# Page slots chosen by readiness, one page more, and the gated half's idle tags put to use, in a two-layer linear-attention and gMLP kernel

## The chip, the core and the metric

The program runs on one core of a Trainium2 chip. The core has a matrix engine (TensorE, PE in the profile; its weight loads are PEld), three elementwise engines (VectorE or DVE, ScalarE or ACT, GpSimd or POOL), a sync engine (SP) that mostly issues DMAs, and 16 DMA engines. Each engine takes its instructions in order; semaphores hold an instruction back until what it needs is done, and whoever stands behind it on that engine waits too. Matmuls write to PSUM (8 banks); all other tiles lie in SBUF.

The metric is the device time of one execution in microseconds, here the median of several runs.

## The reference

Two layers, each an attention block (A) and a gated MLP block (B), all in float32, on 2048 tokens of 512 features:

```python
def _A_ref(x, wqkv, wo):                       # 32 heads of 16
    q, k, v = split(x @ wqkv)
    phi = lambda t: where(t > 0, t + 1, exp(t)) + 1e-6
    pq, pk = phi(q), phi(k)
    kv = einsum("bhsd,bhse->bhde", pk, v)
    z = einsum("bhsd->bhd", pk)
    num = einsum("bhqd,bhde->bhqe", pq, kv)
    den = einsum("bhqd,bhd->bhq", pq, z)[..., None] + 1e-6
    return (num / den) merged @ wo

def _B_ref(x, w_in, w_sp, b_sp, w_out):        # 1792 = 2 x 896 hidden features
    z = gelu(x @ w_in)
    z1, z2 = z[..., :896], layernorm(z[..., 896:])
    g = einsum("ts,bsf->btf", w_sp, z2) + b_sp[None, :, None]
    return (z1 * g) @ w_out

x = x + _A_ref(layernorm(x)); x = x + _B_ref(layernorm(x))   # twice
```

## The kernel before

**Arithmetic.** Every operand of a large product is split into a high part (an ACT copy to fp32r, `high`, L133) and a low part (a DVE subtraction, `low`, L136), and a product is three matmuls (`mm3`, L147 to L149). The big product with `w_sp` (2048 x 2048) and parts of the product with `w_in` are done with fewer products by block sums, so sums and differences of blocks of `w_sp` and `w_in` have to be made; they depend on the weights alone and are stored in DRAM.

**Tokens.** The 2048 tokens are 16 tiles of 128 (`NT`), and each stage runs over them in steps `s` or `i`.

**Stages of a layer.** `P1` (layer norm, keys, the sum G over tokens, queries), `transition` (the 16 x 16 head matrices folded into one 512 x 512 matrix), `P2` (called the gated half below: attention output, residual, layer norm, the first MLP product with gelu, layer norm of its second half), then `P4` (the product with `w_sp`, the gate, the product with `w_out`). The first layer's P1 (`first`) loads and normalises x; the second's (`second`) gets rows that P4 has normalised.

**Rows turned through DRAM.** Matmuls need the features on the partitions. Class `Turn` does this for most tiles by a store to DRAM (L313), a load in another order (L317, by way of L129) and a DVE transposition into a fresh page (L328).

**SBUF slots.** `main` holds 22 pages (`pg`, 128 x 512 floats each), 6 quads, 4 bigs, and 16 tags `z0` to `z15`, one for each token tile. A z tag carries the tile's queries from P1 to P2 (read last by `a2_mul(i)`, in P2's step i − 2), and from P2's step i + 3 on its gelu output z (`e2`). In between nothing is in it. `Slots` hands pages out as a queue: `put` appends a slot to the end of the free list in program order, `get` takes the slot at its head (L48), whatever was done to it last. The tile framework adds the waits: whoever writes into a slot waits for everything that still reads or writes its last content, a store's landing included. `put` comes right behind the emission of a page's last use, for a store right behind the issue of its DMA.

**A step of the gated half** (`P2.run`, from L1074) emits for its engines in this order from step 7 on: loads of x and of a turned row of the attention output (SP); `b_high(s)` and `b_low(s)`, which take three pages, y (L328), h (L133) and l (L136); `c`, a product (TensorE), `c2` (DVE, L835), `c_stats` (DVE, then three small GpSimd operations L266, L267, L271); `a2_mul`; `c3` (ACT normalise, L277, into a fresh page, then a turn through DRAM); `a` (GpSimd); `d_high` and `d_low` (the turned row split into a quad, ACT L133 and DVE L136 on qd); `e4`, `e(s − 3)` (24 matmuls on 448 columns) and `e2` (gelu, L893), `e3` (statistics), up to two `f()` (12 matmuls each, gelu L918, store L921), `side`, and then in the first layer

- `make.step(s)`: class `Make` builds the block sums of `w_in` in three groups, group g beginning at step `MAKE_AT[g]`: fetch (two loads), one step later `add` (four DVE operations, L213 to L216), then two splits and four stores (L228) to `win1_sums`;
- `sums.tick(s, TOKEN_TICKS)`: class `Sums` builds sums of `w_sp` blocks: three loads one step ahead, three GpSimd additions (L1188) at a tick, three stores (L1183) one step later. Eight of them fall into the first layer's gated half, the others into P4 (`MIX_TICKS`).

The second layer's gated half has neither; it runs `Inner.staged` there, block sums inside a block of `w_sp`, on DVE and ACT.

**A step of the first layer's keys** (`P1.first`, from L576): loads, `x_high`, `T_high` (takes y, h), `K` (12 matmuls), `x_low`, `T_low` (l), `K_phi` (r), for ten steps also `Q` (12 matmuls), one or two pieces of the side weights, `K_high`, `Inner.staged` in `ROW_UNITS`, `K_low` (L436), which adds r into the running sum zacc on GpSimd (L440) and gives the old zacc's page back (L441), then `ln_b`, and `Gmm(s − 2)` (12 matmuls), which gives four pages back.

**Constants.** `ident`, `mask` (block diagonal, loaded at the start by L503) and `ones` are tiles of their own; `ones` is the stationary operand of the start's warm-up matmuls (L511) and of the sum over tokens of zacc in `transition` (L705), `mask` is used there too (L726).

Of the kernel before, what the change touches and what calls it, by code (L numbers as in the profile page):

```python
# [36 lines left out]
class Slots:  # L37


    def __init__(self, pool, prefix, n):  # L40
        self.pool, self.prefix = pool, prefix
        self.free_list = deque(range(n))
        self.held = {}
        self.count = 0

    def get(self, shape, dtype=F32):
        assert self.free_list, f"no {self.prefix} slot"
        n = self.free_list.popleft()  # L48
# [5 lines left out]
    def put(self, *tiles):  # L54
        for t in tiles:
            n, _ = self.held.pop(id(t))
            self.free_list.append(n)


class Views:  # L60
# [14 lines left out]
    def put(self, t):  # L75
        if id(t) not in self.held:
            self.pages.put(t)
            return
# [7 lines left out]
def mixer_kernel(ctx: ExitStack, tc: tile.TileContext, x_in, wqkv, wo_d, win1_d, win2_d, wsp_d, bsp_d, wout_d,  # L86
# [9 lines left out]
    pages = Slots(main, "pg", 22)  # L96
# [17 lines left out]
    nc.vector.tensor_copy(ones, ones_f)  # L114
# [36 lines left out]
    class Weight:  # L151
# [13 lines left out]
        def piece(self, pool=False, lows=None):  # L165
# [15 lines left out]
            if lows is None:  # L181
                split(h, l, src, pool)
                pages.put(r)
# [17 lines left out]
    class Make:  # L201
# [22 lines left out]
        def store(self, g):  # L224
# [4 lines left out]
            pages.put(p, l)  # L229
# [103 lines left out]
    class P1:  # L333
# [28 lines left out]
        def send(self, i):  # L362
# [4 lines left out]
            pages.put(self.y)  # L367
# [65 lines left out]
        def K_low(self, i):  # L433
# [5 lines left out]
            else:  # L439
                nc.gpsimd.tensor_tensor(r, self.zacc, r, op=OP.add)  # L440
                pages.put(self.zacc)  # L441
# [50 lines left out]
        def start(self):  # L492

            nc.gpsimd.affine_select(ident, ones_f, pattern=[[1, P]], compare_op=OP.is_equal, fill=0.0, base=0,
# [11 lines left out]
            nc.vector.tensor_copy(m, f)  # L506
            b = banks.get(PAGE)

            def idle(n):
                for _ in range(n):  # L510
                    nc.tensor.matmul(b, ones, m, start=True, stop=True)  # L511
# [17 lines left out]
            pages.put(m, f)  # L529
# [41 lines left out]
        def first(self, side):  # L571
# [3 lines left out]
            own.home = Views(pages, *spare)  # L575
            for s in range(1, NT + 2):  # L576
# [56 lines left out]
        def second(self, side):  # L633
# [4 lines left out]
            for s in range(1, NT + 2):  # L638
# [41 lines left out]
                if s >= 4 and side:  # L680
                    side[0].fetch()
                if s == NT - 1:
                    own.home.close()
# [7 lines left out]
    def transition(p1, p2):  # L691
        wv, wo = p1.wv, p1.wo
        zh, zl = pages.get(PAGE, F32R), pages.get(PAGE, F32R)
# [3 lines left out]
        pages.put(za)  # L697
# [38 lines left out]
        pages.put(m)  # L736
# [1157 lines left out]
```

## Time and profile before

| what | us |
|---|---|
| median of 3 runs (1389.72 to 1391.08) | 1390.81 |
| the profiled execution | 1388.77 |
| its span, first to last instruction | 1387.1 |
| TensorE busy | 1365.0 |
| from the first layer's start to its head matrices (zb, L705) | 135.8 |
| its gated half, with the head matrices | to 371.0 |
| its P4 | to 715.1 |
| the second layer's keys | to 835.6 |
| its gated half, with the head matrices | to 1050.9 |
| its P4, to the end | to 1387.1 |

In the profile, `pg`, `qd`, `bg`, `bank` are pages, quads, bigs and PSUM banks, `z_q` and `z_z` are z tags with queries and with z; `s`, `z`, `n`, `x`, `qt`, `yt`, `xt`, `win_sums` are DRAM tiles (block sums, gelu output, inner sums, x, turned rows of three kinds, sums of `w_in`). `out<-in` names what an instruction writes and reads. A wait `A <- B` reads: A could start only when B was done. `SPq` and the like are an engine's sequencer, which issues DMAs and waits. A matmul's duration there is modelled from its start; the spacing of starts tells the rate.

### The profile page before, as it was taken

What the parts mean: (1) busy time and instruction counts of PE and PEld (TensorE: products, weight loads), DVE (VectorE), ACT (ScalarE), POOL (GpSimd) and SP (SyncE); (2) the same over time, 40 slices, a digit from 0 to 9 for tenths busy, and PEclk for the clock granted to TensorE, in tenths of its full rate; (3) what the DMA queues carried; (4) which work ended last, traced back from release to release, by engine and by line L of the source; (5) the groups of instructions that cost most, each with busy time, mean ns of one, the idle gap of its engine ahead of it and who ended that gap; (6) DMA issues with size and microseconds to landing.
All of it is one profiled execution on the core that took longest, in us unless ns stands there. A gap on an engine that the chain in (4) does not pass through costs nothing.

```text
span 1387.1 us, 18361 instructions
## 1 busy us (share of the span) xinstructions
PE 1365.0 (98%) x6087; PEld 1132.7 (82%) x6087; DVE 1032.3 (74%) x1581; ACT 638.2 (46%) x1021; POOL 470.4 (34%) x551
## 2 busy tenths in 40 slices
PE   9999999988999999999999999999999999999998
PEld 7877888777778888888888888888888888888887
DVE  6885897666765889996578767977776799878742
ACT  6775544344453343343356655543455534533410
POOL 2333474434324325534531124633240011312250
PEclk9999999999999999999999999999999999999999
DMA  5673377876687898896677542666567798658652
GB/s 184 198 217 117 93 242 246 267 236 206 221 280 271 287 316 260 285 330 229 218 248 229 180 150 65 206 200 221 184 205 252 243 333 320 211 187 301 233 183 90
DMA packets 184352, 310.11 MB, mean 224 GB/s; under 512 B 15680, under 2 KB 67776, under 8 KB 180160
## 3 DMA queue, kind: packets, MB, share of 16 engines
q1 hardware_dynamic: 172592, 262.66, 57.5%
q0 software_dynamic: 8064, 39.85, 8.2%
q10 hardware_dynamic: 3600, 6.42, 1.2%
q8 instruction: 48, 0.79, 0.2%
q14 instruction: 48, 0.39, 0.1%
HBM read 211.62 MB, written 97.26 MB: 223 GB/s over the span
## 4 chain that ended last, share of the span: by engine, by line
PE 75%; DVE 8%; DMA 6%; ACT 5%; issue 2%; POOL 2%; SPq 1%; ACTq 0%; DVEq 0%; POOLq 0%
PE bank L149 11%; PE bank L147 11%; PE bank L148 11%; PE bank L1595 9%; PE bank L1596 9%; PE bank L1594 9%; PE bank L1527 3%; PE bank L1528 3%; PE bank L1525 3%; DVE st L262 1%; DVE pg L136 1%; DVE pg L328 1%; PE bank L983 1%; PE bank L985 1%; PE bank L984 1%
## 5 line engine op out<-in xcount | busy, mean ns | idle before, releaser
L1595 PE MATMUL bank<-qd,pg 128*128 128x512 f32 x544 | 211.7, 389 | 0.8 <-DVE qd L1441 0.8
L1596 PE MATMUL bank<-qd,pg 128*128 128x512 f32 x544 | 211.6, 389 | 0.0
L1594 PE MATMUL bank<-qd,pg 128*128 128x512 f32 x544 | 211.6, 389 | 0.0
L1441 DVE TENSOR_TENSOR qd<-qd,qd 128x1024 fp32r<-128x1024 f32 x104 | 142.6, 1372 | 66.2 <-ACT qd L1432 66.0
L1432 ACT ACTIVATE qd<-qd 128x1024 fp32r<-128x1024 f32 x104 | 110.3, 1060 | 127.5 <-DVE qd L1441 45.7
L133 ACT ACTIVATE pg<-pg 128x512 fp32r<-128x512 f32 (+1 forms) x146 | 90.2, 622 | 142.7 <-DVE pg L328 41.9
L149 PE MATMUL bank<-qd,pg 128*128 128x512 f32 x380 | 149.6, 394 | 0.8 <-DVE pg L136 0.8
L1188 POOL TENSOR_TENSOR pg<-pg,pg 128x512 f32<-128x512 f32 x64 | 94.6, 1478 | 137.4 <-DMA pg<-in_wsp_dram 118.1
L266 POOL TENSOR_SCALAR rs<-mv 128x1 f32<-128x1 f32 x95 | 42.1, 444 | 286.6 <-DVE mv L264 274.9
L1616 POOL TENSOR_TENSOR bg<-bg,pg 128x512 f32<-128x512 f32 x56 | 91.1, 1638 | 109.0 <-DMA pg<-z 61.9
L277 ACT ACTIVATE pg<-pg,nb,rs 128x512 f32<-128x512 f32 x63 | 51.3, 815 | 162.0 <-POOL nb L271 161.7
L136 DVE TENSOR_TENSOR pg<-pg,pg 128x512 fp32r<-128x512 f32 (+1 forms) x143 | 106.5, 745 | 22.7 <-ACT pg L133 13.6
L1595 PEld LDWEIGHTS bank<-qd,pg 128*128 128x128 f32 x544 | 102.1, 188 | 22.6 <-DVE qd L1441 1.2
L1594 PEld LDWEIGHTS bank<-qd,pg 128*128 128x128 f32 x544 | 102.1, 188 | 21.4
L1596 PEld LDWEIGHTS bank<-qd,pg 128*128 128x128 f32 x544 | 102.1, 188 | 20.9
L147 PE MATMUL bank<-qd,pg 128*128 128x512 f32 x284 | 111.1, 391 | 0.6 <-ACT pg L133 0.6
L148 PE MATMUL bank<-qd,pg 128*128 128x512 f32 x284 | 110.6, 390 | 0.0
L147 PE MATMUL bank<-bg,qd 128*128 128x448 f32 x256 | 95.6, 374 | 8.5 <-ACT qd L133 8.5
L328 DVE STREAM_TRANSPOSE pg<-pg 128x512 f32<-128x512 f32 x79 | 85.9, 1087 | 17.5 <-DMA z<-pg 6.1
L149 PE MATMUL bank<-bg,qd 128*128 128x448 f32 x256 | 95.4, 373 | 0.2
L148 PE MATMUL bank<-bg,qd 128*128 128x448 f32 x256 | 94.8, 370 | 0.0
L149 PEld LDWEIGHTS bank<-qd,pg 128*128 128x128 f32 x380 | 71.3, 188 | 21.0 <-DVE pg L136 6.4
(214 smaller groups left out, 3235.9 us busy)
## 6 DMA issues: line engine op xcount, KB each, us to landing
qd<-s SPq DMA_DIRECT2D x64, 512.0 KB, 4.0
qd<-n POOLq DMA_DIRECT2D x32, 1024.0 KB, 7.9
pg<-in_wsp_dram SPq DMA_DIRECT2D x95, 256.0 KB, 4.6
qd<-in_wsp_dram SPq DMA_DIRECT2D x40, 512.0 KB, 4.3
s<-pg SPq DMA_DIRECT2D x64, 256.0 KB, 4.4
pg<-z SPq DMA_DIRECT2D x56, 256.0 KB, 3.9
n<-pg SPq DMA_DIRECT2D x54, 256.0 KB, 4.4
x<-pg SPq DMA_DIRECT2D x48, 256.0 KB, 2.6
```

Source lines behind the costliest of these rows:

```text
L136: nc.vector.tensor_sub(l, src, h.bitcast(F32))
L147: nc.tensor.matmul(out, ah, bh, start=start, stop=False)
L148: nc.tensor.matmul(out, ah, bl, start=False, stop=False)
L149: nc.tensor.matmul(out, al, bh, start=False, stop=stop)
L328: nc.vector.transpose(y.rearrange("p c (t m) -> p m c t", m=4), r.rearrange("p (m c j) -> p m c j", m=4, c=4))
L1188: nc.gpsimd.tensor_tensor(t, a, b, op=OP.add)
L1432: nc.scalar.activation(wh, r, AF.Copy)
L1441: nc.vector.tensor_sub(wl, r, wh.bitcast(F32))
L1594: m(out, h[:, o], w[:, 0, j, :], start=start, stop=False, skip_group_check=True)
L1595: m(out, h[:, o], w[:, 1, j, :], start=False, stop=False, skip_group_check=True)
L1596: m(out, l[:, o], w[:, 0, j, :], start=False, stop=stop, skip_group_check=True)
L1616: nc.gpsimd.tensor_tensor(u, u, z1, op=OP.mult)
```

## The change

Five things.

1. **Slots by readiness.** The free list holds pairs (count, slot). `put` files a slot under the number of gets so far plus a lag: 0 where an engine other than GpSimd used it last, `POOL` = 3 where GpSimd reads it, `STORE` = 6 where a store does. `get` takes the lowest number.
2. **One page more**, 23; to make room `mask`, `ones` and `ones_f` are no longer tiles of their own, and `den` rotates over 2 buffers rather than 4. The warm-up matmuls use slices of one page of ones; `mask` and `ones` get two pages late in P1, step 15, where the mask is loaded and, in step 16, the ones are made from it by one DVE operation; `transition` gives both back.
3. **Block-sum operands in idle z tags.** `TOKEN_TICKS` becomes a dictionary from the step to the tags that the operands of its sum take; what has no tag takes a page.
4. **Turned rows in idle z tags.** `c3(i)` normalises into tag z[i − 1] rather than into a page where the row is turned through DRAM; both layers.
5. **Times.** The last two sums of the gated half move from steps 14 and 17 to 13 and 14; `MAKE_AT` from 7, 10, 12 to 5, 8, 11; the inner sums of the first layer's keys begin before step 1 and run in steps 1 to 8; the second side piece a step begins at step 9 rather than 10.

```diff
-TOKEN_TICKS = (5, 6, 8, 9, 11, 12, 14, 17)
+STORE, POOL = 6, 3
+TOKEN_TICKS = {5: (5, 6), 6: (7,), 8: (8, 9), 9: (10,), 11: (11, 12), 12: (13,), 13: (14,), 14: (15,)}
-MAKE_AT = 7, 10, 12
-ROW_UNITS = range(2, 10)
+MAKE_AT = 5, 8, 11
+ROW_UNITS = range(1, 9)
...
-        self.free_list = deque(range(n))
+        self.free_list = [(0, i) for i in range(n)]
...
-        n = self.free_list.popleft()
+        first = min(self.free_list, key=lambda e: e[0])
+        self.free_list.remove(first)
+        n = first[1]
...
-    def put(self, *tiles):
+    def put(self, *tiles, lag=0):
         for t in tiles:
             n, _ = self.held.pop(id(t))
-            self.free_list.append(n)
+            self.free_list.append((self.count + lag, n))
...
-    pages = Slots(main, "pg", 22)
+    pages = Slots(main, "pg", 23)
...
-    mask = consts.tile([P, P], F32, name="mask")
-    ones_f = consts.tile([P, P], F32, name="ones_f")
+    ones_f = pages.get(PAGE)
     nc.vector.memset(ones_f, 1.0)
-    ones = consts.tile([P, P], F32R, name="ones")
-    nc.vector.tensor_copy(ones, ones_f)
...
-                pages.put(self.zacc)
+                pages.put(self.zacc, lag=POOL)
...
-            nc.sync.dma_start(mask, mask_d)
-            m, f = pages.get(PAGE, F32R), pages.get(PAGE)
-            nc.vector.memset(f, 1.0)
-            nc.vector.tensor_copy(m, f)
+            m = pages.get(PAGE, F32R)
+            nc.vector.tensor_copy(m, ones_f)
...
+            own.begin(2, 1)
             for s in range(1, NT + 2):
...
-                        for _ in range(min(len(side), 1 if s < 10 else 2)):
+                        for _ in range(min(len(side), 1 if s < 9 else 2)):
...
-                for w in list(side)[:1 if s < 9 else 2]:
+                for w in list(side)[:1 if s < 8 else 2]:
                     w.fetch()
-                if s == 1:
-                    own.begin(2, 1)
+                if s == NT:
+                    nc.vector.tensor_scalar(self.ones, self.mask, 0.0, 1.0, op0=OP.mult, op1=OP.add)
                 if s == NT - 1:
+                    self.pair = pages.get(PAGE, F32R), pages.get(PAGE)
+                    self.ones, self.mask = (t[:, 0:P] for t in self.pair)
+                    nc.sync.dma_start(self.mask, mask_d)
...
-        pages.put(m)
+        pages.put(m, *p1.pair)
...
-            den = small.tile([P, 32], F32, name="den")
+            den = small.tile([P, 32], F32, name="den", bufs=2)
...
-            y = pages.get(PAGE)
             turned = self.xturn.turned(i)
+            y = ztag(i - 1, PAGE, "turn") if turned else pages.get(PAGE)
             normalise(feats(y, turned), feats(x, False), self.ms.pop(i))
-            pages.put(x)
+            pages.put(x, lag=STORE)
             self.xturn.store(i, y)
-            if i in self.xturn.by_pe:
+            if not turned:
                 self.xB[i] = y
-            else:
-                pages.put(y)
...
-        def fetch(self):
+        def fetch(self, tags=()):
...
+                raw, tags = [], deque(tags)
+                for n, s in ((j, k), (j, k + HT), (2 + j, k)):
+                    t = ztag(tags.popleft(), PAGE, "sum") if tags else pages.get(PAGE)
+                    nc.sync.dma_start(t, wsp_d[n, s])
+                    raw.append(t)
+                self.raw.append(raw)
```

The second layer's `second` gets the same lines for the pair of pages. `lag=STORE` is added at the other puts that follow a store (`Make.store`, `P1.send`, `a2_mul`, `f`, `gelu_out`, `Sums.store`, `Inner.out`, the last lines of `P4.o`), `lag=POOL` at those behind a GpSimd read (weight pieces split on GpSimd, zacc in `transition`, `gates`). `affine_select` for `ident` reads a slice of the page of ones.

More of the change, by code (lines that the diff above doesn't have):

```diff
@@ L182, in piece @@
                 split(h, l, src, pool)
-                pages.put(r)
+                pages.put(r, lag=POOL if pool else 0)
             else:
@@ L366, in send @@
             self.kept_d[i] = self.turn.d[i]
-            pages.put(self.y)
+            pages.put(self.y, lag=STORE)
         def ln_a(self, i):
@@ L510, in idle @@
                 for _ in range(n):
-                    nc.tensor.matmul(b, ones, m, start=True, stop=True)
+                    nc.tensor.matmul(b, m[:, 0:P], m, start=True, stop=True)
             idle(9)
@@ L528, in start @@
             banks.put(b)
-            pages.put(m, f)
+            pages.put(m, ones_f)
             self.T_low(0)
@@ L681, in second @@
                     side[0].fetch()
+                if s == NT:
+                    nc.vector.tensor_scalar(self.ones, self.mask, 0.0, 1.0, op0=OP.mult, op1=OP.add)
                 if s == NT - 1:
+                    self.pair = pages.get(PAGE, F32R), pages.get(PAGE)
+                    self.ones, self.mask = (t[:, 0:P] for t in self.pair)
+                    nc.sync.dma_start(self.mask, mask_d)
                     own.home.close()
@@ L692, in transition @@
         wv, wo = p1.wv, p1.wo
+        ones, mask = p1.ones, p1.mask
         zh, zl = pages.get(PAGE, F32R), pages.get(PAGE, F32R)
@@ L696, in transition @@
         split(zh, zl, za, True)
-        pages.put(za)
+        pages.put(za, lag=POOL)
         p1.late()
@@ L921, in f @@
             nc.sync.dma_start(z1s[self.L, n, f], t)
-            pages.put(t)
+            pages.put(t, lag=STORE)
             return True
@@ L928, in gelu_out @@
             nc.scalar.dma_start(z1s[self.L, n, f], t)
-            pages.put(t)
+            pages.put(t, lag=STORE)
         def block_sums(self):
@@ L1183, in store @@
                 nc.sync.dma_start(self.s[m, k][:, j, :], t)
-                pages.put(t, *done)
+                for t in (t, *done):
+                    if id(t) in pages.held:
+                        pages.put(t, lag=STORE)
             self.made = []
@@ L1616, in gates @@
                 nc.gpsimd.tensor_tensor(u, u, z1, op=OP.mult)
-                pages.put(z1)
+                pages.put(z1, lag=POOL)
             self.loaded = []
@@ L1729, in o @@
             else:
-                pages.put(x)
+                pages.put(x, lag=STORE)
             if i % 4 == 3:
```

17 lines of the change are left out of this document (8 added, 9 removed).

## The prediction

> **What bounds the kernel now.** I read the page first (engine shares, chain), then the busy time of every engine by stretch, then the waits by engine in the stretch that stood out, then the instructions there in order of time.
>
> ```profile
> span 1387.1 us, 18361 instructions
> PE 1365.0 (98%) x6087; PEld 1132.7 (82%) x6087; DVE 1032.3 (74%) x1581; ACT 638.2 (46%) x1021; POOL 470.4 (34%) x551
> PE 75%; DVE 8%; DMA 6%; ACT 5%; issue 2%; POOL 2%; SPq 1%; ACTq 0%; DVEq 0%; POOLq 0%
> ```
>
> TensorE sets the time; nothing in the change adds or removes a matmul of the computation, so only stretches where TensorE is held up can pay. They are found by comparing twin stretches. The gated half (class P2) runs once per layer with the same 985 matmuls:
>
> ```profile
> 139.79:371.02 231.23, 218.81 (x985) 183.09 (x984) 173.83 (x299) 102.80 (x170) 110.24 (x153) 0.99 0.67 218
> 839.57:1050.91 211.34, 211.09 (x985) 181.92 (x984) 162.80 (x294) 104.32 (x172) 79.36 (x129) 1.00 0.58 187
> ```
>
> The columns are length, then busy time and instructions of PE, PEld, DVE, ACT, POOL, then clock, DMA share, GB/s. The first layer takes 231.23 − 211.34 = **19.9 us longer**. Who held TensorE, and what held those engines, from 160 to 371 us (total, times, longest):
>
> ```profile
> PE bank L147 <- ACT qd L133: 8.5, 4, 3.8
> DVE pg L136 <- DMA s<-pg: 3.2, 2, 2.2
> DVE pg L328 <- DMA z<-pg: 3.2, 2, 2.2
> DVE pg L328 <- DMA win_sums<-pg: 2.7, 1, 2.7
> DVE pg L136 <- DMA z<-pg: 2.1, 1, 2.1
> DVE pg L940 <- DMA z<-pg: 1.9, 1, 1.9
> ACT pg L133 <- DMA z<-pg: 5.4, 2, 4.2
> ```
>
> The last six are waits of an engine for a store to land that has nothing to do with its data: it wants to write into a page whose last content is still on its way out. DVE 13.1 us, ACT 5.4 us. One case in order of time, step 11 of the loop:
>
> ```profile
> 249.49 0.62 ACT L133 ACTIVATE qd<-pg 128x512 fp32r<-128x512 f32 x1
> 253.95 1.16 SPq L228 DMA_DIRECT2D win_sums<-pg  x2
> 256.68 1.52 SPq L1183 DMA_DIRECT2D s<-pg  x3
> 256.93 1.08 DVE L328 STREAM_TRANSPOSE pg<-pg 128x512 f32<-128x512 f32 x1 [2.69 <-DMA win_sums<-pg]
> 258.09 0.63 ACT L133 ACTIVATE pg<-pg 128x512 fp32r<-128x512 f32 x1 [4.61 <-DVE pg L328]
> 261.28 0.69 DVE L136 TENSOR_TENSOR pg<-pg,pg 128x512 fp32r<-128x512 f32 x1 [2.17 <-DMA s<-pg]
> 265.95 0.62 ACT L133 ACTIVATE qd<-pg 128x512 fp32r<-128x512 f32 x1
> 266.62 0.47 PE L147 MATMUL bank<-bg,qd 128*128 128x448 f32 x1 [2.03 <-ACT qd L133]
> ```
>
> Going through the gets and puts of the code in program order, the three pages that b() takes in step 11 were given back by Make.store, Make.store and Sums.store, eight to ten gets earlier, and these gets bunch at the end of a step; at b_low the free list holds three pages in steps 6, 9, 12 and 13. So the queue hands out exactly the pages whose stores were just issued. ACT's copy for the next e() slips from 249.49 to 265.95, 16.46 us, and TensorE waits 2.03 us for it.
>
> **The second place** is steps 13 to 16 of the first layer's keys (P1.first), where a step has only 24 matmuls:
>
> ```profile
> DVE pg L328 <- POOL pg L440: 4.2, 3, 1.4
> 101.11 1.09 DVE L328 STREAM_TRANSPOSE pg<-pg 128x512 f32<-128x512 f32 x1 [1.41 <-POOL pg L440]
> sum 27.16, PE 25.18 PEld 17.09 DVE 18.65 ACT 16.90 POOL 8.87; mean PE 6.29 PEld 4.27 DVE 4.66 ACT 4.22 POOL 2.22
> 390.00:420.00 30.00, 30.00 (x134) 24.83 (x133) 17.02 (x20) 15.04 (x22) 11.96 (x8) 1.00 0.88 289
> ```
>
> The sum row closes four windows of one step each between 92.28 and 119.44. At the undisturbed rate of the last row, 30.00/133 = 0.2256 us a matmul, four steps need 96 × 0.2256 = 21.7 us; they take 27.2, **5.5 us too long**. The transposed page of step s is, by the queue, the page that K_low gave back in step s − 1, and GpSimd is still reading it.
>
> **The change part by part.**
>
> *Slots by readiness* (get takes the lowest count; a stored page counts six gets late, one that GpSimd reads three), *one page more, and the gated half's idle tags*. In P2 a sum keeps one or two of its three operands in tags z5 to z15, and a turned row goes into z[i−1]. Counted the same way, with Make's earlier steps, the free pages at b_low rise from three, three and five in steps 12 to 14 to five, six and six. Pages that DVE or TensorE gave back go first, so b() comes to pages given back by c3 or a2_mul in the middle of the step before, half a step and more after the issue, against landings of
>
> ```profile
> s<-pg SPq DMA_DIRECT2D x15, 256.0 KB, 4.1
> yt<-pg SPq DMA_DIRECT2D x7, 256.0 KB, 2.3
> ```
>
> All six waits above should go. What is late next? The DVE/ACT chain of a step itself. In step 11 the DVE waits of 2.69 and 2.17 us lie on it, so 16.46 − 4.9 = 11.6 us are left. A full step of TensorE is, between two firsts of e() in the second layer,
>
> ```profile
> 950.57 0.36 PE L147 MATMUL bank<-bg,qd 128*128 128x448 f32 x1
> 963.62 0.36 PE L147 MATMUL bank<-bg,qd 128*128 128x448 f32 x1
> 1010.71 0.63 ACT L133 ACTIVATE qd<-pg 128x512 fp32r<-128x512 f32 x1 [2.30 <-DVE pg L328]
> 1013.93 0.36 PE L147 MATMUL bank<-bg,qd 128*128 128x448 f32 x1
> ```
>
> 13.05 us, so the chain fits. In the short steps at the end (no f() left) the second layer's copy still comes 1013.93 − 1010.71 − 0.63 = 2.6 us ahead of TensorE. The first layer has more to do there: sums now at 11, 12, 13 and 14. Bounds for this term: all of 19.9 (twin), and about 12 (two of the four holes, 2.1 us each, left with 1.7 of slow clock) if the last steps lose what their extra work costs. I take **−16.5**, nearer to the twin, whose chain is the same code.
>
> *TensorE's clock.* After that 2.03 us hole the granted clock was 0.89:
>
> ```profile
> 266.50:281.60 15.10, 14.92 (x60) 12.53 (x61) 11.41 (x20) 6.07 (x11) 7.87 (x10) 0.89 0.77 247
> ```
>
> 0.11 × 15.1 = 1.7 us on top of the hole; this is inside the 19.9. The Trainium skill, "TensorE: Matmul & The Clock Gate", Part 1, has the clock halved only after an idle window of about 3.4 us; here 2.0 us were enough, so the trace decides. By that rule of the Trainium skill only the 3.8 us hole would slow the clock, the four together would cost 10.2 us instead of 15.3, and the first rival below would come to 1378.
>
> *Keys, steps 13 to 16:* zacc's page counts three gets late and falls behind the four pages of Gmm, so DVE's 1.41 us before L328 goes; 3 × 1.41 = 4.2 of the 5.5. Left is a cycle of 27.16/4 − 1.41 = 5.4 us against TensorE's 5.4, no room. Bounds 2 and 5.5; I take **−4.0**.
>
> *Start:* ones, its copy and a second memset shrink to one page memset and one copy.
>
> ```profile
> 1.09 0.23 DVE L114 CAST ones<-ones_f 128x128 fp32r<-128x128 f32 x1
> 1.90 0.43 DVE L506 CAST pg<-pg 128x512 fp32r<-128x512 f32 x1
> 2.38 4.21 PE L511 MATMUL bank<-pg,ones 128*128 128x512 f32 x9 [2.38 <-DVE pg L506]
> 6.39 1.05 PE L289 MATMUL bank<-ident,pg 128*128 128x128 f32 x4
> ```
>
> The warm-up matmuls start some 0.45 us sooner and end sooner, and the first transposes stand right behind them (bounds 0 and −0.45): **−0.3**. The mask leaves SP's start and comes back in step 15 with wv behind it; its load (a quarter of 256 KB, below 4.1 us) has a step of at least 5.4 us before step 16's DVE op, which is like the 0.23 us cast. Twice 0.23, bound 0.5, on a DVE that idles there: 0.
>
> *Moved earlier:* own.begin's two loads now stand ahead of loadx(4) and of step 1's row store on SP; x4 is needed two steps later. The row units, one DVE add and one subtraction of 0.69 us and an ACT copy each, run in steps 1 to 8 rather than 2 to 9, and a second weight piece joins at step 9; a step has 36 matmuls there, 8.1 us, with DVE below it. Make moves two, two and one steps up, with two loads, four adds, two splits and four stores a group:
>
> ```profile
> 270.73 0.42 DVE L216 TENSOR_TENSOR pg<-pg 128x256 f32<-128x256 f32 x1
> 271.25 4.03 POOL L1188 TENSOR_TENSOR pg<-pg,pg 128x512 f32<-128x512 f32 x3
> 274.29 1.54 DVE L136 TENSOR_TENSOR pg<-pg,pg 128x512 fp32r<-128x512 f32 x1
> ```
>
> Four adds are 1.7 us of DVE in one step, covered by the 13.05 − 11.6 us and TensorE's lead; without that cover 1.7 each, 5.1 for three. I keep this cover at 0 and have it in a rival. The sums of steps 14 and 17 move to 13 and 14 with three loads and three stores on SP and 4.03 us of GpSimd; nothing waits for the stores before the next half.
>
> *New waits:* ACT's normalise into z[i−1] waits for a sum's store one step old (z5, z8, z11 only), e2 for the turned row's store. Behind both stand d_high and the gelus, and TensorE behind d_high. The row's store is issued with the normalise and lands in 2.3 us; e2 comes a step, 13 us, later. Bounds 0 and 1 us at three places: **+0.8** for these and what I have not seen.
>
> Sum: −16.5 − 4.0 − 0.3 + 0.8 = **−20.0**. The profiled execution took 1388.77 us (1.67 around its span), 2.0 below the median of 1390.81; its 1368.8 becomes **1370.8** on the median's scale.
>
> **The rivals.**
>
> *Half of it.* Lag is counted in gets, not in time; where frees bunch up, young stores are still handed out. For: the pages that failed in step 11 were eight to ten gets old, more than the lag of six. Against: one to three more free pages, and the second layer's half, which has such waits too and no holes (860 to 1050 us):
>
> ```profile
> ACT pg L133 <- DMA z<-pg: 6.2, 4, 2.6
> ```
> If the four holes (8.5 us) stay with 1.7 of slow clock each, 15.3 of the 19.9 do: −4.6 − 4.0 − 0.3 + 0.8 = −8.1, **1383**.
>
> *GpSimd's sums in four steps running.* Step 12's split took DVE 1.54 us beside L1188 instead of 0.69, and stats' small GpSimd operations queue behind 4.03 us of adds. If steps 11 to 14 lose 2 us each beyond their lead, 8 of the 16.5 are given back: −12, **1379**. The Trainium skill, "SBUF — State Buffer", 🔬 SBUF: two separate sides, says that GpSimd and a DVE operation with two SBUF inputs lock each other out for a whole instruction; it speaks for this rival, and 1.54 against 0.69 agrees.
>
> *Slower: turned rows in the z tags.* The row in z[i−1] must be out before e2 writes there, with ACT in order. If SP's queue (sums' loads, Make's stores) delays that store by more than the 13 − 2.3 us of room, ACT stalls in all twelve turned steps of both layers, and the second layer's half, now free of it, loses what the first loses today: −4.3 + 19.9, **1406**. Against: in step 11 the row's store could follow the normalise at once, SP being through with the 1.16 and 1.52 us of stores by then.
>
> *It does not do what it says:* if at each get only young stores are free, the lowest count is the same page as before: **1390**.
>
> **How the numbers follow.** Forecast 0.56, own range 1366 to 1377 (P2 −12 to −19.9, keys −2 to −5.5); better than that 0.04; half 0.15; GpSimd 0.12; the slower rival 0.09; no effect 0.04. A measurement of this kernel tells about 0.2% (2.8 us) from no change. Faster 0.56 + 0.04 + 0.15 + 0.12 = 0.87, same 0.04, slower 0.09. The range 1365 to 1384 takes in the forecast and the two partial rivals and leaves out about 0.15.
>
> **What would show it.** Right: the first layer's gated half within 5 us of the second's; no wait of L328, L136 or L133 on a store of z, s or win_sums over 1 us there; L328 no longer on L440; steps of 5.4 to 5.7 us in the keys; TensorE's clock 1.00 in both halves. Wrong: waits of L277 or L893 on yt or s, or holes in TensorE in the second layer's gated half. A first layer that loses 5 us or more in steps 11 to 17, with rs of L266 behind L1188, is the GpSimd rival; the same with stores named is the half.

## The result, and the profile after

| | before | changed |
|---|---|---|
| median, us | 1390.74 (1389.72 to 1391.08, 4 runs) | 1373.33 (1371.57 to 1376.9, 4 runs) |
| ratio, 95% interval | | 0.9879 (0.9859 to 0.99) |
| the profiled execution, us | 1388.77 | 1371.57 |

Faster by 17.4 us; 20.0 was forecast. Line numbers shift in the changed kernel: L803 below adds `zeps` to `den`, L1187 and L1194 load and store the block sums, L1201 is GpSimd's add of them.

The page of the changed kernel. Its chain (last line) sums to 78% only, because followed back from the end it breaks off at 284.7 us of the span, so it leaves out most of the first layer's gated half and can't be held against the chain before:

```profile
span 1369.8 us, 18327 instructions
PE 1358.0 (99%) x6087; PEld 1132.0 (83%) x6087; DVE 1024.6 (75%) x1581; ACT 636.7 (46%) x1021; POOL 467.5 (34%) x551
PE 71%; DVE 3%; DMA 2%; issue 1%; ACT 1%; POOL 0%; SPq 0%; DVEq 0%; ACTq 0%; POOLq 0%
```

Busy time by stretch: the two gated halves (columns as before: length, busy time of PE, PEld, DVE, ACT, POOL, then clock, DMA share, GB/s):

```profile
134.33:354.02 219.69, 215.38 (x986) 182.35 (x984) 171.76 (x299) 102.58 (x170) 108.79 (x153) 0.99 0.71 230
821.58:1033.03 211.45, 211.20 (x986) 181.89 (x984) 162.21 (x294) 104.06 (x172) 79.68 (x129) 1.00 0.59 188
```

The first layer's half fell from 231.23 to 219.69, by **11.5 us**; its twin stayed (211.34 to 211.45), so 8.2 us of the gap are still there. The four key steps, as four windows and their sum:

```profile
92.28:97.72 5.44, 5.44 (x25) 4.50 (x24) 4.41 (x8) 3.75 (x7) 1.60 (x5) 1.00 0.69 195
...
sum 21.78, PE 21.78 PEld 17.97 DVE 17.52 ACT 14.72 POOL 8.00; mean PE 5.45 PEld 4.49 DVE 4.38 ACT 3.68 POOL 2.00
```

27.16 became 21.78, **5.4 us** less, and TensorE is busy throughout. Those two places are 16.9 of the 17.2 us between the two profiled executions. The waits in the first layer's gated half, 155 to 354 us (total, times, longest):

```profile
DVE pg L136 <- DMA z<-pg: 3.4, 2, 1.8
...
PE bank L147 <- ACT qd L133: 2.7, 2, 2.0
```

Of the six waits on stores that the prediction listed, one kind is left (L136 behind z, 3.4 us after 2.1), and TensorE's holes before e() fell from 8.5 to 2.7 us. So the time came from where it was expected. Whether it came *by what* was expected is a question for runs that take the change apart.

### The profile page after: what moved, and what is told of

Read it like the earlier page. It is cut to its first block, busy times and chain, and to the rows that moved or that the text cites. A ratio compares the mean times of both kernels' runs of the same rounds, so it can differ in the third digit from the quotient of the medians.

```text
span 1369.8 us, 18327 instructions
## 1 busy us (share of the span) xinstructions
PE 1358.0 (99%) x6087; PEld 1132.0 (83%) x6087; DVE 1024.6 (75%) x1581; ACT 636.7 (46%) x1021; POOL 467.5 (34%) x551
## 4 chain that ended last, share of the span: by engine, by line
PE 71%; DVE 3%; DMA 2%; issue 1%; ACT 1%; POOL 0%; SPq 0%; DVEq 0%; ACTq 0%; POOLq 0%
PE bank L149 11%; PE bank L147 10%; PE bank L148 10%; PE bank L1608 9%; PE bank L1607 9%; PE bank L1609 9%; PE bank L1540 4%; PE bank L1541 4%; PE bank L1538 4%; PE bank L989 1%; PE bank L991 1%; PE bank L990 1%; DMA yt<-z_turn 1%; DMA pg<-yt 0%; DVE st L262 0%
## 5 line engine op out<-in xcount | busy, mean ns | idle before, releaser
L1608 PE MATMUL bank<-qd,pg 128*128 128x512 f32 x544 | 211.7, 389 | 0.5 <-DVE qd L1454 0.5
L1609 PE MATMUL bank<-qd,pg 128*128 128x512 f32 x544 | 211.6, 389 | 0.0
L1607 PE MATMUL bank<-qd,pg 128*128 128x512 f32 x544 | 211.6, 389 | 0.0
L149 PE MATMUL bank<-qd,pg 128*128 128x512 f32 x380 | 149.0, 392 | 0.5 <-DVE pg L136 0.4
L136 DVE TENSOR_TENSOR pg<-pg,pg 128x512 fp32r<-128x512 f32 (+1 forms) x143 | 108.4, 759 | 20.4 <-ACT pg L133 15.8
L1608 PEld LDWEIGHTS bank<-qd,pg 128*128 128x128 f32 x544 | 102.1, 188 | 22.1 <-DVE qd L1454 0.9
L1607 PEld LDWEIGHTS bank<-qd,pg 128*128 128x128 f32 x544 | 102.1, 188 | 21.2
L1609 PEld LDWEIGHTS bank<-qd,pg 128*128 128x128 f32 x544 | 102.1, 188 | 21.2
L1201 POOL TENSOR_TENSOR pg<-pg,pg 128x512 f32<-128x512 f32 x45 | 67.3, 1495 | 137.6 <-DMA pg<-in_wsp_dram 116.8
L147 PE MATMUL bank<-qd,pg 128*128 128x512 f32 x284 | 110.9, 391 | 0.5 <-ACT pg L133 0.5
L148 PE MATMUL bank<-qd,pg 128*128 128x512 f32 x284 | 110.6, 390 | 0.0
L328 DVE STREAM_TRANSPOSE pg<-pg 128x512 f32<-128x512 f32 x79 | 86.0, 1088 | 6.0 <-DMA pg<-yt 2.9
L1540 PE MATMUL bank<-qd,pg 128*128 128x512 f32 x224 | 87.4, 390 | 0.3 <-DVE qd L1454 0.3
L1538 PE MATMUL bank<-qd,pg 128*128 128x512 f32 x224 | 87.2, 389 | 0.0
```

The source lines that it names most:

```text
L136: nc.vector.tensor_sub(l, src, h.bitcast(F32))
L147: nc.tensor.matmul(out, ah, bh, start=start, stop=False)
L148: nc.tensor.matmul(out, ah, bl, start=False, stop=False)
L149: nc.tensor.matmul(out, al, bh, start=False, stop=stop)
L1538: m(out[i], h[:, o, f], w[:, o, 0], start=first and name in ("P1", "P2", "P5"), stop=False, skip_group_check=True)
L1540: m(out[i], h[:, o, f], w[:, o, 1], start=False, stop=False, skip_group_check=True)
```

## The experiments

Every row is a kernel of its own, compared with the kernel before on the same chip. The last two columns come from the one profiled execution of each: the four key steps (TensorE's matmuls 384 to 480), and the first layer's gated half. How far such columns repeat can be read from the second layer's half, which no edit here takes work out of: from its first to its last e() it took 159.2 to 159.7 us in all fourteen profiles.

| kernel | median, us | ratio, 95% interval | key steps | gated half |
|---|---|---|---|---|
| before | 1390.74 | 1 | 27.16 | 231.23 |
| changed | 1373.33 | 0.9879 (0.9859 to 0.99) | 21.78 | 219.69 |
| plain queue, 23 pages | 1375.02 | 0.9879 (0.9865 to 0.9894) | 22.94 | 221.47 |
| readiness, 22 pages | 1376.08 | 0.9891 (0.9876 to 0.9906) | 23.41 | 219.81 |
| plain queue, 22 pages | 1377.79 | 0.9904 (0.9889 to 0.9919) | 25.66 | 220.19 |
| store lag 12 | 1375.4 | 0.9885 (0.9869 to 0.9902) | 22.57 | 219.45 |
| plain queue, 22 pages, tags only | 1384.15 | 0.9955 (0.994 to 0.997) | 26.37 | 226.30 |
| plain queue, 22 pages, times only | 1386.79 | 0.997 (0.9959 to 0.9982) | 25.97 | 229.43 |
| Make at 6, 9, 12 | 1378.64 | 0.9916 (0.9901 to 0.9931) | 22.68 | 224.12 |
| sums behind the next loads on SP | 1377.38 | 0.9907 (0.9892 to 0.9922) | 22.48 | 222.97 |
| sums at 3, 4, 5, 7, 8, 10, 11, 13 | 1376.69 | 0.9902 (0.9886 to 0.9919) | 22.42 | 220.98 |
| without GpSimd's adds | 1370.14 | 0.9857 (0.9843 to 0.9872) | 22.95 | 217.27 |
| without Make's adds | 1371.86 | 0.9866 (0.9851 to 0.9881) | 21.81 | 217.61 |
| one operand of three loaded | 1371.39 | 0.985 (0.9831 to 0.9868) | 22.93 | 216.19 |

### Is it readiness? Three kernels without it, without the page, without both

```diff
-STORE, POOL = 6, 3
+STORE, POOL = 0, 0
```

With both lags at 0 the pairs are sorted by the order of the puts, which is the old queue.

> The changed kernel with both lags at 0, so that every get takes the oldest free page as before; the 23rd page, the tags and the new times stay. Readiness theory (the prediction's): the keys' 4 to 5 us come back, because zacc's page no longer stands behind the others, with L328 waiting on L440 again, and the first layer's gated half loses 6 us or more: about 1384. Rival, page count: counted in program order, with 23 pages even the plain queue gives L328 in the keys a page that GpSimd does not read, and b() in steps 9 to 14 pages of the same kinds as with lags; no wait on L440, gated half within 2 us of the changed kernel: 1372 to 1376.

```diff
-    pages = Slots(main, "pg", 23)
+    pages = Slots(main, "pg", 22)
```

> The changed kernel with 22 pages; lags, tags and times stay. Readiness theory: keys unchanged (zacc's page goes to others), gated half loses at most 2 us: 1374 to 1376. Page count rival: in steps 9 and 12 both b_high and b_low now get pages whose z stores were issued at the end of the step before (ten gets old), instead of b_low alone; waits of ACT L133 and DVE L136 on DMA z come back over 4 us in all and two TensorE holes of about 2 us with slow clock after them, 4 to 8 us: 1378 to 1382.

Both edits together:

> The changed kernel with 22 pages and both lags at 0; only the tags and the new times are left of the change. Both theories have the keys' wait of L328 on L440 back (the transposed page is again the one that K_low gave back), plus 4 to 5 us. Readiness theory: the gated half is as in the run with 23 pages and no lags, 1383 to 1386. Page count rival: gated half as in the run with 22 pages and lags: 1382 to 1387, and 8 us or more above the run with 23 pages and no lags.

Readiness is worth nothing that can be measured while there are 23 pages (0.9879 against 0.9879, each known to some 2 to 3 us), and the kernel with neither keeps four fifths of the gain (0.9904; 13.4 us), where both theories had expected 1382 us or more. What it loses, it loses in the keys. Its waits from 60 to 138 us, and the four key steps as windows:

```profile
DVE pg L328 <- POOL pg L440: 4.2, 3, 1.4
```

```profile
93.12:98.71 5.59, 5.59 (x26) 4.43 (x24) 4.60 (x8) 3.82 (x7) 2.35 (x4) 1.00 0.60 174
98.71:105.38 6.67, 6.31 (x26) 4.27 (x24) 4.35 (x8) 3.71 (x7) 2.35 (x4) 1.00 0.61 185
105.38:112.08 6.70, 6.33 (x26) 4.27 (x24) 4.37 (x8) 3.72 (x7) 2.36 (x4) 1.00 0.30 79
112.08:118.78 6.70, 6.33 (x26) 4.27 (x24) 3.95 (x6) 3.98 (x7) 1.30 (x1) 1.00 0.48 123
```

The wait is the one of the kernel before, to the tenth, and each of the three steps that have it is 1.25 us longer than the 5.44 us of the changed kernel. Either cure works alone (22.94 and 23.41 us in the table, and of the 4.2 us of waiting on L440 0.7 and nothing are left): the lag moves zacc's page behind others, and the 23rd page moves the whole queue on by one, so that, counted in program order, L328 gets the page that T_low gave back. In the gated half neither matters much: 1.8 us in the one profile with 23 pages and the plain queue (221.47), and with both taken away only 0.5. There the kernel without both shows, from 160 to 359 us,

```profile
ACT pg L133 <- DMA z<-pg: 14.6, 3, 5.4
...
PE bank L147 <- ACT qd L133: 3.7, 3, 2.0
```

ACT waits nearly three times as long for young z stores as in the kernel before (5.4 us), and the half is 0.5 us longer than the changed kernel's (220.19 against 219.69). So ACT's copy in b_high has room here; the rows of before named waits of ACT and of DVE, and they don't weigh the same. The page count rival overstated the page (it had 4 to 8 us for 22 pages with lags; 219.81 against 219.69 was measured), readiness overstated the order.

### Do young stores hold the rest?

```diff
-STORE, POOL = 6, 3
+STORE, POOL = 12, 3
```

> The changed kernel with a store counted twelve gets late instead of six. If young stores that are still handed out to b_low in steps 9 and 12 hold up the rest of the gated half (3.4, 2 and 1.8 us of DVE waits on DMA z there), these waits go and the holes after 282 and 306 us shrink: 1369 to 1372. If the rest is the chain of DVE and ACT beside GpSimd's adds and the slower landings, nothing changes: 1372 to 1375.

The waits of L136 on z are gone, and the half is the same, 219.45 us. The rival "half of it" falls: what is left of the gap is not pages with young stores. (One new wait stands there: in step 13 ACT's normalise starts at 284.65, when a sum's store has left its tag, 1.0 us after its factors are ready. A gain of that size could be hidden by it.)

### Tags or times?

Both on the plain queue with 22 pages. Tags only: Make back to 7, 10, 12, and the last two sums back to 14 (with z15) and 17 (pages). Times only: every sum operand and every turned row in pages.

```diff
-TOKEN_TICKS = {5: (5, 6), 6: (7,), 8: (8, 9), 9: (10,), 11: (11, 12), 12: (13,), 13: (14,), 14: (15,)}
-MAKE_AT = 5, 8, 11
+TOKEN_TICKS = {5: (5, 6), 6: (7,), 8: (8, 9), 9: (10,), 11: (11, 12), 12: (13,), 14: (15,), 17: ()}
+MAKE_AT = 7, 10, 12
```

> 22 pages, plain queue, with the tags for the sums' operands and the turned rows, but Make at steps 7, 10, 12 and the last two sums at 14 and 17 as before: of the gated half's edits the tags alone. The kernel with 22 pages, plain queue, tags and new times took 1377.8. Theory tags (they free pages, so b() gets fewer young stores): 1377 to 1381, gated half of layer 1 below 229 us. Theory times (Make and the sums of 14 and 17 stood in the short steps at the end, where TensorE has no lead): 1384 to 1390, gated half above 229.

```diff
-TOKEN_TICKS = {5: (5, 6), 6: (7,), 8: (8, 9), 9: (10,), 11: (11, 12), 12: (13,), 13: (14,), 14: (15,)}
+TOKEN_TICKS = (5, 6, 8, 9, 11, 12, 13, 14)
...
-            y = ztag(i - 1, PAGE, "turn") if turned else pages.get(PAGE)
+            y = pages.get(PAGE)
...
-            if not turned:
-                self.xB[i] = y
+            if turned:
+                pages.put(y, lag=STORE)
+            else:
+                self.xB[i] = y
```

> 22 pages, plain queue, no tags at all (sums' operands and turned rows in pages), Make at 5, 8, 11 and the sums at 5, 6, 8, 9, 11 to 14 as in the changed kernel: of the gated half's edits the times alone. Counted in program order the free pages fall to one, and b() in steps 6, 9 and 12 to 14 gets pages with stores of the step before throughout. Theory tags: waits of L328, L133 and L136 on stores of s, z and win_sums over 10 us in all, holes in TensorE as before or more: 1386 to 1394. Theory times: such waits come, but the chain has lead in the middle steps: 1378 to 1382.

The gated half, before 231.23: tags alone take off 4.9 us, times alone 1.8, both 11.0. The parts need each other. Without tags the free pages run down to one, and DVE waits as never before (times only, 160 to 368 us):

```profile
DVE pg L328 <- DMA win_sums<-pg: 12.8, 3, 4.8
...
DVE pg L328 <- DMA z<-pg: 3.9, 3, 1.9
```

Without the new times two holes at the end of the half stay (before, 2.03 and 3.80 us). TensorE in order of time, tags only:

```profile
290.82 0.47 PE L147 MATMUL bank<-bg,qd 128*128 128x448 f32 x1 [3.04 <-ACT qd L133]
...
324.19 0.47 PE L147 MATMUL bank<-bg,qd 128*128 128x448 f32 x1 [3.74 <-ACT qd L133]
```

and the changed kernel:

```profile
284.70 0.47 PE L147 MATMUL bank<-bg,qd 128*128 128x448 f32 x1 [2.01 <-ACT qd L133]
...
307.04 0.47 PE L147 MATMUL bank<-bg,qd 128*128 128x448 f32 x1 [0.66 <-ACT qd L133]
```

The 3.8 us hole of before is the one at 324 here: Make's last group and two sums stood in steps 13 to 17, where a step of TensorE is short.

### What is left: 8.2 us, and three tries to get them

The step that ends in the hole at 284.70, changed kernel, DVE and GpSimd in order of time:

```profile
273.26 0.42 DVE L214 TENSOR_TENSOR pg<-pg,pg 128x256 f32<-128x256 f32 x1
...
276.12 1.28 DVE L803 TENSOR_TENSOR den<-den,zeps 128x32 f32<-128x32 f32 x1
277.43 0.35 DVE L804 RECIPROCAL den<-den 128x32 f32<-128x32 f32 x1
279.38 0.69 DVE L136 TENSOR_TENSOR pg<-pg,pg 128x512 fp32r<-128x512 f32 x1 [1.59 <-DMA z<-pg]
```

```profile
276.06 1.29 POOL L1201 TENSOR_TENSOR z_sum<-z_sum,pg 128x512 f32<-128x512 f32 x1
```

L213 to L216 are Make's adds, DVE's own; an operation on 32 columns takes as long as GpSimd's whole add beside it, and the step is 14.60 us from copy to copy (269.43 to 284.03) against 13.05 of TensorE. The first try keeps the two apart by moving Make, the second keeps SP's queue clear for the turned rows, the third moves the sums:

```diff
-MAKE_AT = 5, 8, 11
+MAKE_AT = 6, 9, 12
```

> The changed kernel with Make at 6, 9, 12, so that its four DVE adds stand in steps 7, 10 and 13, of which 7 and 10 have no block sum. If the rest of the loss is the step chain in steps that hold both a sum and Make's adds (14.6 us from copy to copy against 13.05 of TensorE at 190 and 269 us, GpSimd's adds beside them), steps 6, 9 and 12 lose 2 us of chain and the holes after 282 and 306 us (2.0 and 0.8, with 2 us of slow clock) mostly go: 1368 to 1371. If the loss is set by the sum of the work of steps 5 to 14, it only moves later: 1372 to 1376.

```diff
                 self.loadx(s + 1)
                 self.qturn.load(s + 1)
+                if self.L == 0:
+                    sums.tick(s - 1, TOKEN_TICKS)
...
-                if self.L == 0:
-                    sums.tick(s, TOKEN_TICKS)
```

> The changed kernel with the sums' SP work (three stores, three loads a step) issued behind the next step's loads of x and of the turned q row instead of ahead of them; the adds of GpSimd keep their order. If the hole after 306 us comes from the q row's load standing behind the sums' transfers on SP (issued at 295.3, landed 300.3, L328 waits for it until 301.6), that hole (0.8 us) and part of the lag before it go: 1370.5 to 1372.5. If the chain of DVE sets it: unchanged within 1 us of 1373.3.

```diff
-TOKEN_TICKS = {5: (5, 6), 6: (7,), 8: (8, 9), 9: (10,), 11: (11, 12), 12: (13,), 13: (14,), 14: (15,)}
+TOKEN_TICKS = {3: (), 4: (), 5: (5, 6), 7: (7,), 8: (8, 9), 10: (10,), 11: (11, 12), 13: (13,)}
```

> The changed kernel with its block sums at 3, 4, 5, 7, 8, 10, 11, 13: no step holds both Make's four adds and a sum, and counted in program order b_low in steps 9 and 12 finds seven free pages instead of five, none with a store of the step before. If it is the two on one chain that use up the lead (steps from copy to copy of 14.6 us at 190 and 269 us against 13.05), the chain stays below 13.5 us in every step, the holes after 282 and 306 us go, half 214 to 217 us: 1368 to 1371. If the sums cost the same wherever they stand: 1372 to 1375. If the sums' loads and stores at 3 and 4 delay the early steps, whose rows TensorE turns: above 1375.

All three are slower, and the first two by more than either theory allowed. Make one step later costs 4.4 us of the half (TensorE's holes before e() grow from 2.7 to 6.6 us), as with the later times of "tags only". Sums at 3 and 4 cost the lead in the steps that turn their rows on TensorE, whose steps are short too: where the long steps begin, the copy for e() is 1.4 us ahead of it instead of 5.4. And behind the next step's loads the sums' stores come so late that the rival of the turned rows is seen at work (157 to 359 us):

```profile
ACT z_turn L277 <- DMA s<-z_sum: 23.1, 3, 9.3
...
PE bank L147 <- ACT qd L133: 6.1, 3, 4.3
```

ACT may not write row s − 1 into its tag before the sum that lay there is out. In the changed kernel this wait decides nothing, by half a microsecond: in step 13 the store landed at 282.74, the row's factors were ready at 283.28.

### What is left, taken apart

```diff
+            if m == 4:
-            nc.gpsimd.tensor_tensor(t, a, b, op=OP.add)
+                nc.gpsimd.tensor_tensor(t, a, b, op=OP.add)
```

> The changed kernel without GpSimd's 24 block-sum adds in the first layer's gated half: the operands are loaded and stored as before, but not added, so what reads the sums reads unsummed blocks. The first layer's gated half took 219.7 us from the first product, the second layer's, without sums, 211.3. Theory GpSimd: its adds slow the chain of each step (a DVE operation on 32 columns took 1.28 us beside them, and stats' small operations queue behind them); without them the half takes 213 to 216 us: 1367 to 1370. Theory Make (DVE's own four adds a group, 2.1 us on the chain of three steps): at most 2 us less, 1371 to 1373.

```diff
-            nc.vector.tensor_add(A22, A21, A22)
-            nc.vector.tensor_sub(A21, A11, A21)
-            nc.vector.tensor_sub(A11, A22, A11)
-            nc.vector.tensor_sub(A12, A12, A11)
+            pass
```

> The changed kernel without the four DVE adds of Make.add in each of its three groups; what is split and stored are the loaded blocks, so the sums of the input weight are missing. Theory Make: steps 6, 9 and 12 are 2.1 us of chain shorter, 6.3 in all; the lead of the copy for e() over TensorE does not run out at 282 us, and the half takes 214 to 217 us: 1368 to 1371. Theory GpSimd: at most 2 us less, 1371 to 1373.

```diff
-                    nc.sync.dma_start(t, wsp_d[n, s])
+                    if not raw:
+                        nc.sync.dma_start(t, wsp_d[n, s])
...
-                self.add(1, k, j, a22, a21, a22)
-                self.add(3, k, j, a21, a21, a11)
-                self.add(2, k, j, a11, a22, a11)
+                self.add(1, k, j, a22, a21, a21)
+                self.add(3, k, j, a11, a21, a22)
+                self.add(2, k, j, a21, a22, a11)
```

> The changed kernel with one of the three operands of each block sum loaded in the first layer's gated half; the three GpSimd adds and three stores of a sum stay, but the sums are made of that one operand, so two loads of 256 KB a sum, 16 in all, are left out. Theory DMA (what is left of the loss in that half is the queue of transfers: the turned rows' stores there took 4.2 us to land in the mean against 2.8 in the second layer, in bursts that land 0.65 us apart): in eight steps 1.3 us less stand ahead of the rows, lead is kept, the half takes 214 to 217.5 us against 219.7: 1367 to 1371. Theory chain (DVE, ACT and GpSimd alone set it, each part with some 2 us as measured): within 1 us of the changed kernel's 1373.3.

The half by windows, without GpSimd's adds, and with one load of three:

```profile
136.05:353.32 217.27, 213.72 (x986) 181.20 (x984) 161.19 (x298) 102.90 (x170) 77.73 (x129) 1.00 0.72 232
```

```profile
137.67:353.86 216.19, 213.35 (x986) 181.35 (x985) 171.71 (x299) 102.63 (x170) 108.00 (x153) 1.00 0.68 215
```

Without the adds the half is 2.4 us shorter, without Make's adds 2.1, with two loads of three left out 3.5. (Without the adds and with one load, the edit reaches the eight sums in P4 too; TensorE doesn't wait there, and only the half is compared.) Only the loads reach the range expected of them. That the three add up to 8.0 of the 8.2 us is no proof that they are its parts: all three kernels lose the same hole. The 2.01 us at 284.70 are 0.37, 1.08 and 0.52 us there, and the slow clock behind it, worth 1.65 us (last section), is gone each time. So TensorE's busy time falls by 1.7, 1.8 and 2.0 us in the three, and its idle time by 0.8, 0.2 and 1.5 us. With any one taken out, 4.7 to 6.2 us of the gap stay; no run takes out two, and the shares stay open.

The loads count most, and the trace shows what they may do. Median time from issue to landing, changed kernel, 180 to 335 us:

```profile
yt<-z_turn SPq DMA_DIRECT2D x12, 256.0 KB, 4.3
```

the same in the second layer, 860 to 1013 us, and in the first with one load of three:

```profile
yt<-z_turn SPq DMA_DIRECT2D x12, 256.0 KB, 2.4
```

```profile
yt<-z_turn SPq DMA_DIRECT2D x12, 256.0 KB, 2.3
```

How the queue fills is seen in SP's own row of time in the changed kernel:

```profile
269.55 0.37 SPq L313 DMA_DIRECT2D yt<-z_turn  x1
275.63 0.32 SPq L129 DMA_DIRECT2D pg<-yt  x1
276.05 0.86 SPq L927 DMA_DIRECT2D z<-pg  x2
276.96 1.15 SPq L228 DMA_DIRECT2D win_sums<-pg  x2
278.20 1.62 SPq L1194 DMA_DIRECT2D s<-z_sum  x2
279.87 0.83 SPq L1194 DMA_DIRECT2D s<-pg  x1
280.76 0.64 SPq L1187 DMA_DIRECT2D z_sum<-in_wsp_dram  x1
281.49 1.13 SPq L1187 DMA_DIRECT2D pg<-in_wsp_dram  x2
...
284.69 0.57 SPq L313 DMA_DIRECT2D yt<-z_turn  x1
290.18 0.32 SPq L129 DMA_DIRECT2D pg<-yt  x1
```

SP waits some 5 us for the turned row to land, then issues all that has gathered (15 transfers of 256 KB in 8.6 us, four of them not shown, the next row's store last), and that row goes in behind the others: 284.69 to 290.16, 5.5 us. The Trainium skill, "DMA: Bandwidth & Descriptors", 🔬 Anatomy of one DMA — SWDGE (gpsimd) path, has a transfer on GpSimd's path take about 2.0 us and a part that grows with the bytes, by its fit 2.6 us for 256 KB, an estimate; SP issues the rows here, for which that fit isn't made, and their 2.4 us in the second layer lie near it.

The landing of the row is not the whole cause, though. Without GpSimd's adds it is 5.2 us, longer than the changed kernel's 4.3, and the half is 2.4 us shorter; in the kernel before and in "times only" it is 2.3 us in the first layer too, with longer halves. Nor does the run tell the transfers from SP's time to issue them, and it leaves out loads alone: that a sum's store has a price because the next row stands behind it is argued from SP's order, not measured.

## Why the prediction was right, and where it was not

- **What bounds the kernel, and the two places: right.** The gated half gave 11.5 us and the key steps 5.4 in the profiled execution, nothing measurable came from elsewhere.
- **"All six waits above should go", by readiness, the page and the tags: most went, by the tags and the new times alone.** With the plain queue and 22 pages DVE's five kinds are gone, ACT's has grown to 14.6 us, and 11.0 of the 11.5 us in the half are there. The tags free enough pages for DVE, and the new times, which the sum kept at 0 ("Moved earlier", "I keep this cover at 0"), empty the short steps at the end; 6.1 of the 11.0 us come only with them (226.30 to 220.19). That the total fell into the range is thus in part luck: in the half, what was named first paid next to nothing, and a term put at 0 paid.
- **The mis-sized term: the gated half at −16.5, measured −11.5**, just outside its bound of "about 12". It was set nearer to the twin because the twin's chain is the same code. The twin has none of the sums' six transfers a step, and no adds of Make and of GpSimd: the step that failed is to take these as free, "three loads and three stores on SP and 4.03 us of GpSimd; nothing waits for the stores" and the cover of "1.7 each" kept at 0. Leaving out 16 of those loads, GpSimd's adds or Make's adds shortens the half by 3.5, 2.4 or 2.1 us, 1.7 to 2.0 of it each time in TensorE's busy time, which goes with one slow clock. The 2.3 us for a turned row, true of the kernel before, became 4.3.
- **The clock.** The prediction put 1.7 us of slow clock behind each of the four holes. In the kernel before, only two have it, that of 2.03 us at 266.62 and that of 3.80 us at 328.97; behind 295.52, also 2.03 us, the clock is 1.00. So the 15.3 us of "half of it" were 3.4 too many.
- **The GpSimd rival** had its mechanism right (without the adds DVE is busy 161.19 us instead of 171.76, as in the second layer), at a third of its price: 10.6 us less of DVE shorten the half by 2.4. By the Trainium skill, "SBUF — State Buffer", 🔬 SBUF: two separate sides, a DVE operation with two SBUF inputs and a GpSimd operation that reads SBUF lock each other out for a whole instruction; L803's 1.28 us beside L1201's 1.29 agrees.
- **"Half of it"** is refuted by the store lag of 12. **"Turned rows"** did not happen in this kernel, but it stands half a microsecond away, and the second layer, where no sum lies in the tags, is untouched.
- **Keys: −4.0 predicted, right in place and size, by two cures instead of one.** Seven kernels run the changed kernel's instructions up to there; their key steps take 21.78 to 22.95 us, 22.4 in the mean, so 4.7 us is the better figure, and the profiled execution of the changed kernel was the luckiest of them. Two things make it less. The three kernels with neither cure take 25.66 to 26.37 us and not 27.16, so some 3.6 us belong to the cures. And in five of the seven the fifth step loses again (5.94 to 7.02 us against 5.50 before), where L328 waits up to 2.6 us for a row's load; over five steps the seven save 4.0 us in the mean. Why that load lands late, no run shows.
- **Start: −0.3, and "moved earlier" 0.** The warm-up starts 0.41 us sooner, and at step 13 of the keys nothing of it is left: both kernels begin the first of the four steps at 92.28 us. By the trace the inner sums, one step earlier, give it back: a copy waits for their store, and the step with that wait takes 9.26 us against 8.16 before (9.06 to 9.76 in the twelve other kernels, which all have the new steps). Changed kernel:

```profile
1.97 4.21 PE L509 MATMUL bank<-pg 128*128 128x512 f32 x9 [1.97 <-DVE pg L504]
...
60.28 0.63 ACT L133 ACTIVATE qd<-qd 128x512 fp32r<-128x512 f32 x1 [2.09 <-DMA n<-qd]
...
64.67 0.50 PE L147 MATMUL bank<-qd,pg 128*128 128x512 f32 x1 [0.53 <-ACT pg L133]
```

- **The total** came out nearer than its largest term. By stages the profiles give −11.5 for the half and −4.7 for the keys, 16.2 us (15.5 with the fifth step); the median's 17.4 (13.9 to 19.6 by the interval of the ratio) agrees with either. Of the signs named, "steps of 5.4 to 5.7 us" and "L328 no longer on L440" came true; "within 5 us of the second's", "no wait over 1 us" (1.8 was left) and "clock 1.00 in both halves" (0.99) did not.

No version tried beats the changed kernel with the whole computation.

## What to carry to other kernels

When a wait on a buffer shows, ask first how many buffers are free there, and only then which one is handed out: with 23 pages the order was worth nothing that could be measured, with 22 it still took one wait away (the keys' 25.66 us became 23.41). What order does for the half without the tags, no run shows. Don't weigh such a wait by its length but by the engine that has it: with 14.6 us on ACT the half was half a microsecond longer, 1.41 us on DVE cost 1.25 us each time. A transfer that TensorE's chain doesn't need can still have a price, as 16 loads did here (3.5 us); compare twin stretches only after their queues have been compared. And when parts are taken away one at a time, look whether they remove the same hole before adding up what each gave.

## What the hardware showed beside that

The length of a hole alone doesn't say whether TensorE's clock falls. Behind the 2.01 us hole at 284.70 of the changed kernel it was 0.89 over the next 15 us:

```profile
284.66:299.66 15.00, 14.90 (x62) 12.92 (x63) 10.17 (x16) 7.85 (x13) 7.31 (x11) 0.89 0.86 291
```

0.11 × 15.0 = 1.65 us on top of the hole. With 22 pages and the plain queue the clock stayed whole behind a hole just as long (TensorE in order of time, then the window behind it):

```profile
290.07 0.47 PE L147 MATMUL bank<-bg,qd 128*128 128x448 f32 x1 [2.03 <-ACT qd L133]
```

```profile
290.07:305.07 15.00, 13.61 (x60) 10.90 (x61) 10.38 (x16) 7.69 (x13) 6.84 (x10) 1.00 0.89 297
```

From 20 us on, the fourteen traces have nine holes of 2.00 to 2.03 us: five are followed by 0.89 and four by 1.00, one of each in the kernel before. (The one with 23 pages and the plain queue has another, of 1.68 us, 4.6 us ahead of it.) The five of 2.77 to 4.27 us all have a slow clock behind them (0.80 to 0.89 over 15 us), one of 2.51 us has none, nor have the seven of 1.21 to 1.45 us. With one profile of each kernel it stays open whether the changed kernel's 1.65 us come in every execution. The other surprise is how far profiles of the same instructions lie apart: up to the head matrices the seven kernels named above took 130.4 to 133.7 us, a spread of 3.3 us in a stretch whose gain is 3.7 in the mean (from 135.8).
